# Attention with a top-32 mask and a feed-forward behind it: other places for values, feed-forward items and masking in each engine's queue

## The chip, the core and the metric

The kernel runs on one NeuronCore of one Trainium2 chip. Five engines with queues of their own work side by side: TensorE (PE; its weight loads are listed as PEld), VectorE (DVE), ScalarE (ACT), GpSimd (POOL) and SyncE (SP, which issues most transfers here). Each engine takes its instructions in the order in which the program issued them; an instruction that waits for another engine holds up all that stand behind it on its own. The metric is the device time of one execution in microseconds, as the median of several runs.

## What is computed

Eight batches of eight heads of attention, 576 rows of 64 each, keep the 32 largest scores of a row; the outcome goes through a feed-forward with the activation h - tanh(h). The weights come as 64-bit floats, all else is 32-bit.

```python
# q, k, v: (8, 8, 576, 64) float32
scores = scale * np.matmul(q, k.transpose(0, 1, 3, 2))
kth = np.partition(scores, -32, axis=-1)[..., -32:-31]
scores = np.where(scores >= kth, scores, -1e9)
attn = np.exp(scores - np.max(scores, axis=-1, keepdims=True))
attn = attn / (np.sum(attn, axis=-1, keepdims=True) + 1e-09)
x = np.matmul(attn, v)           # to (4608, 512): batch and row, then head and column
h = x @ w_in                     # (512, 2048)
return (h - np.tanh(h)) @ w_out  # (2048, 512)
```

## The kernel before

**Steps.** The attention is cut into 144 steps. A step is one pair of heads and a block of 128 rows (a `Step`); the 64 rows that are left over of each head make steps of their own, with two pairs of heads together (`rem`). The first batch, 18 steps, has `pe` set: its masked scores are transposed on PE. In the others DVE transposes them in blocks of 32 and 16 transfers on SP put the blocks in place (`turn_z`, `spread_keys`).

**What happens to a step n.** The work is spread over several turns of the loop in `run`, so that in each turn several steps are in the air:
- `scores(n)`, in turn n - 1: PE multiplies queries and keys into the one PSUM tile `scps`, ACT copies it to `sc`.
- `search(n)`, in turn n: DVE takes the minimum and maximum of two halves (L267, L268; these read `scps` and `sc` and write `ab`), then four rounds of the eight largest (L275) and their removal (L278). After each round `between` lets other work in: the conversion of weights (`convert`, L157 to L172, in turns 0 to 10 alone), transposes of keys and queries (L222), `turn_z`.
- `mask(n)`, in turn n + 1: POOL makes the threshold `tb` (L294) and the bias `nb` (L303); ACT computes a large value where a score is below the threshold (L307), POOL subtracts it (L310), once for each head. POOL then looks, from `ab`, whether a row may have been searched wrongly (`bad`, L314). `ab` has two buffers, so the search after the next one needs it.
- `expo(n)`, in turn n + 1: ACT takes the exponentials and their sums (L330), POOL adds a small number (L340).
- `turn_pe(n)`, in turn n + 2, for `pe` steps: nine transposes on PE (L409), eight at once and one behind `next(w)`, and ACT's copies to `et` (L412).
- `spread(n)`: POOL repeats the inverted sums along 64 columns (`rx`, L355).
- `values(n)`, in turn n + 2 for `pe` steps and n + 4 for the others, after the last step of a pair (or the only one): PE multiplies `et` with the values (L433), two heads beside each other in 64 columns, and transposes `rx` (L441); ACT copies both to `xs` (L445) and POOL multiplies them into `xT` (L457). `et` has one buffer: the next transfers into it wait until these matmuls have read it.

**The feed-forward.** Rows are gathered into units of 256 (128 at the start and for left-over rows). When the last values of a unit are made, its items are appended to the list `work`: `ffn_h` items (L486, 16 matmuls of 128 columns or 8 of 256 each in the program), of which each second one ends a PSUM tile `hps` that ACT turns into tanh (L498) and a copy `g` (L499) and POOL into `g` minus tanh (L500); then `ffn_o` items (L507, two matmuls of 512 columns), of which each eighth ends with ACT's copy `ot` (L517) and the transfer out. In the trace a float32 matmul stands as two instructions.

**Dealing.** `rate` looks at the number of items in `work` and at the turns in which later units will be ready, and says how many items this turn should do (`share`). `deal(part)` adds that part of the share to a credit and takes so many items from the list. The parts of a turn add up to 1.

**The order of a turn**, which sets the order in every queue: `spread(n - 3)`; `values`; `share`; the first eight transposes of `turn_pe(n - 2)`; `mask(n - 1)`; `search(n)`; `spread_keys(n - 2)`; for `pe` steps `spread(n - 2)`; `deal(0.4)`; `scores(n + 1)`; the ninth transpose; `expo(n - 1)`; `deal(0.2)`; `values(n - 2)` for `pe` steps; `deal(0.2)`; loads that are due; `deal(0.2)`. After the last turn the rest of the items follows in a row.

The pools matter where they make something wait: `scps` one tile; `zt` (which holds zt and av) two; `hps` and `ops` two together; `th` four, shared by tanh, `ot` and the conversion's `f`.

Of the kernel before, what the change touches and what calls it, by code (L numbers as in the profile page):

```python
# [8 lines left out]
AF = mybir.ActivationFunctionType  # L9
ALU = mybir.AluOpType  # L10
FP32 = mybir.dt.float32
# [5 lines left out]
BIG = 2.0**80  # L17
# [31 lines left out]
def kernel(  # L49
# [9 lines left out]
    nc = tc.nc  # L59
    P = nc.NUM_PARTITIONS  # L60
    B, H, S, D = q.shape
# [9 lines left out]
    NG = P // G  # L71
    KC = 2 * S // P
    G = 32
    NG = P // G
# [17 lines left out]
    zpool = pool("z", 2)  # L92
# [191 lines left out]
    def mask(n, exact):  # L284

        x = st[n]
        sc, m = x["sc"], x.pop("m")
        scf = sc[:].rearrange("p t s k -> p t (s k)")
        tb = mpool.tile([P, 2], FP32, tag="tb", name="tb")
        if exact:  # L290
            nc.gpsimd.tensor_scalar(tb[:], m[:, :, TOP - 1], BIG, None, ALU.mult)
        else:
            for t in range(2):
                nc.gpsimd.tensor_scalar(  # L294
                    tb[:, t : t + 1],
                    m[:, t, TOP - 1 : TOP],
                    m[:, t, TOP - 9 : TOP - 8],
                    BIG,
                    ALU.min,
                    ALU.mult,  # L300
                )
        nb = mpool.tile([P, 2], FP32, tag="nb", name="nb")
        nc.gpsimd.tensor_scalar(nb[:], m[:, :, 0], -scale, None, ALU.mult)  # L303
        z = zpool.tile([P, 2 * S], FP32, tag="z", name="z")
        zv = z[:].rearrange("p (t k) -> p t k", t=2)
        for t in range(2):
            nc.scalar.activation(  # L307
                zv[:, t, :], scf[:, t, :], AF.Relu, bias=tb[:, t : t + 1], scale=-BIG
            )
            nc.gpsimd.tensor_tensor(zv[:, t, :], scf[:, t, :], zv[:, t, :], ALU.subtract)  # L310
        if not exact:
            ab = x.pop("ab")
            for t in range(2):
                nc.gpsimd.tensor_scalar(  # L314
                    bad[:, t, n : n + 1],
                    ab[:, t, S2 + 7 : S2 + 8],
                    BIG,
                    tb[:, t : t + 1],
                    ALU.mult,
                    ALU.is_gt,  # L320
                )
        x.update(z=z, zv=zv, nb=nb)

    rds = {}
# [94 lines left out]
    def values(n):  # L419

        g = steps[n]
        nq, u = g.nq, g.unit
        et = tiles(ets.pop(n), nq)
        rx = rxs.pop(n)
        w = nq * P
        av = zt_ps.tile([P, 2, N], FP32, tag="zt", name="av")
        for i in range(2 if g.rem else 1):
            cols = half(i) if g.rem else slice(0, w)
            es = et[:, 2 * i : 2 * i + 2] if g.rem else et
            hp = g.hp + i  # L430
            for c in range(J + 1):
                for t in range(2):
                    nc.tensor.matmul(  # L433
                        av[half(t), 0, cols],
                        vb[g.b, hp][:, t, c, :] if c < J else vr[g.b, hp][:, t, :],
                        es[:, :, (J + 1) * t + c if c < J else J].rearrange("p a i j -> p a (i j)"),
                        start=(c == 0),
                        stop=(c == J),
                    )
        for i in range(nq):  # L440
            nc.tensor.transpose(  # L441
                av[:, 1, 0:w].rearrange("p (a i j) -> p i a j", a=NG, i=nq)[:, i], rx[:, i].rearrange("p t d -> p (t d)"), ident[:]
            )
        xs = xrpool.tile([P, 2, N], FP32, tag="xs", name="xs")
        nc.scalar.copy(xs[:, :, 0:w], av[:, :, 0:w])  # L445
        if g.rem:
            for i in range(2):
                nc.gpsimd.tensor_tensor(
                    xt(u)[:, g.hp + i, g.col : g.col + R],
                    xs[:, 0, half(i)],  # L450
                    xs[:, 1, half(i)],
                    ALU.mult,
                )
        else:

            xv = xs[:, :, 0:w].rearrange("p s (a i j) -> p s i a j", a=NG, i=nq)
            nc.gpsimd.tensor_tensor(  # L457
                xt(u)[:, g.hp, g.col : g.col + w].rearrange("p (i a j) -> p i a j", a=NG, i=nq),
                xv[:, 0],
                xv[:, 1],  # L460
                ALU.mult,
            )
        if n in done:
            work.extend(ffn(u))
# [6 lines left out]
            u.xT = p.tile([P, CD, N], FP32, tag=u.tag, name=u.tag)  # L471
        return u.xT

    cur = {}

    def ffn_h(u, item):

        w = u.n
        per = 2 * P // w
        for f in range(item * per, (item + 1) * per):  # L480
            j, fo = f // FJ, (f % FJ) * P
            s = f * w % 512
            if s == 0:
                cur[u] = h_ps.tile([P, 512], FP32, tag="h", name="hps")
            for c in range(CD):
                nc.tensor.matmul(  # L486
                    cur[u][:, s : s + w],
                    w_in[j][:, c, fo : fo + P],
                    u.xT[:, c, 0:w],
                    start=(c == 0),  # L490
                    stop=(c == CD - 1),
                )
        if item % 2:
            th = thpool.tile([P, 512], FP32, tag="th", name="th")
            if item % 4 == 1:
                u.g.append(gpool.tile([P, 2, 512], FP32, tag="g", name="g"))
            g = u.g[-1][:, item % 4 // 2, :]
            nc.scalar.activation(th[:], cur[u][:], AF.Tanh)  # L498
            nc.scalar.copy(g, cur[u][:])  # L499
            nc.gpsimd.tensor_tensor(g, g, th[:], ALU.subtract)  # L500

    def ffn_o(u, i, part):
        if part == 0:
            cur[u] = h_ps.tile([P, DM], FP32, tag="h", name="ops")
        for f in range(2 * part, 2 * part + 2):
            o = f * u.n + i * P
            nc.tensor.matmul(  # L507
                cur[u][:],
                u.g[o // 1024][:, o % 1024 // 512, o % 512 : o % 512 + P],
                w_out[f // FJ][:, f % FJ, :],  # L510
                start=(f == 0),
                stop=(f == CF - 1),
            )
        if part < CF // 2 - 1:
            return
        ot = thpool.tile([P, DM], FP32, tag="th", name="ot")
        nc.scalar.copy(ot[:], cur[u][:])  # L517
        for rows, dst in u.blocks[i]:
            nc.sync.dma_start(dst, ot[rows, :])
# [50 lines left out]
    def run(exact):  # L570
# [67 lines left out]
        def here(i):  # L638
            return 0 <= n + i < NS
# [24 lines left out]
        def rate():  # L664


            have, low, high = len(work), 0.0, None
            coming = sorted((t, u.n // 8) for u, t in ready.items() if t > n)
            for t, k in coming + [(NS + 4, 0)]:
                r = have / max(t - n, 1)  # L670
                high = r if high is None else min(high, r)
                have += k
            for u, t in begun.items():
                if t > n and u in before:
                    need = [i + 1 for i, x in enumerate(work) if x[1] is before[u]]
                    if need:
                        low = max(low, need[-1] / (t - n))
            return max(low, high)
# [11 lines left out]
        for n in range(-4, NS + 4):  # L690
            pe = here(-2) and steps[n - 2].pe
            if here(-3) and not steps[n - 3].pe:
                spread(n - 3)
            for m in (n - 4, n - 3):
                if 0 <= m < NS and steps[m].last and steps[m].lag == n - m:
                    values(m)
            share, usable = rate(), converted[0]
            if pe:
                w = turn_pe(n - 2)
                next(w)  # L700
            if here(-1):
                mask(n - 1, exact)
            if here(0):
                search(n, exact, between)
            elif here(-2):
                between(0)
            if here(-2) and not pe and steps[n - 2].last:
                spread_keys(n - 2)
            if pe:
                spread(n - 2)  # L710
            deal(0.4)
            if here(1):
                scores(n + 1)
            if pe:
                next(w)
            if here(-1):
                expo(n - 1)
            deal(0.2)
            if pe and steps[n - 2].last:
                values(n - 2)  # L720
            deal(0.2)
            for fn in todo.pop(n, []):
                fn()
            deal(0.2)
# [48 lines left out]
```

## Time and profile before

| | us |
|---|---|
| median of 5 runs | 1549.71 (1549.24 to 1550.34) |
| the profiled execution | 1551.08 |
| its span, first to last instruction | 1549.2 |
| PE busy | 1440.5 (93%) |
| DVE busy | 1347.2 (87%) |
| POOL busy | 943.2 (61%) |
| ACT busy | 884.0 (57%) |

Busy time is the time in which at least one record of the engine is open. A matmul's record begins before the one ahead of it has ended, so that PE's busy share can hide pauses of a tenth of a microsecond; how fast PE goes is read from the starts. The largest groups are `ops` on PE (L507, 522.9 us), `hps` on PE (L486, 474.4 us), the maxima on DVE (L275, 472.7 us), POOL's subtraction (L310, 400.5 us) and DVE's removals (L278, 382.6 us).

In the timelines below the columns are start, length, engine, line, operation, written and read tile, shape, count, and in brackets how long the engine had been idle before it and who ended that.

### The profile page before, as it was taken

What the parts mean: (1) busy time and instruction counts of PE and PEld (TensorE: products, weight loads), DVE (VectorE), ACT (ScalarE), POOL (GpSimd) and SP (SyncE); (2) the same over time, 40 slices, a digit from 0 to 9 for tenths busy, and PEclk for the clock granted to TensorE, in tenths of its full rate; (3) what the DMA queues carried; (4) which work ended last, traced back from release to release, by engine and by line L of the source; (5) the groups of instructions that cost most, each with busy time, mean ns of one, the idle gap of its engine ahead of it and who ended that gap; (6) DMA issues with size and microseconds to landing.
All of it is one profiled execution on the core that took longest, in us unless ns stands there. A gap on an engine that the chain in (4) does not pass through costs nothing.

```text
span 1549.2 us, 25298 instructions
## 1 busy us (share of the span) xinstructions
PE 1440.5 (93%) x7428; PEld 913.3 (59%) x7428; DVE 1347.2 (87%) x3828; ACT 884.0 (57%) x1567; POOL 943.2 (61%) x1525
## 2 busy tenths in 40 slices
PE   2566899899999999999999999999999999999997
PEld 1355567455566665656566665656566665656673
DVE  6997889999999999999999999999999999997300
ACT  4886767556555565656565565656565565655320
POOL 2777667667565675657565675757565675746420
PEclk9887899999999999999999999999999999999999
DMA  9944113324443354234433354334443344322200
GB/s 240 363 170 162 50 27 66 92 69 93 109 90 79 81 105 102 70 79 95 107 86 79 81 108 101 70 79 97 100 90 80 80 100 109 81 64 58 74 9 16
DMA packets 258836, 147.42 MB, mean 95 GB/s; under 512 B 210049, under 2 KB 217217, under 8 KB 258689
## 3 DMA queue, kind: packets, MB, share of 16 engines
q1 hardware_dynamic: 256912, 145.49, 38.4%
q8 instruction: 62, 1.02, 0.3%
q14 instruction: 86, 0.70, 0.2%
q10 hardware_dynamic: 1776, 0.22, 0.1%
HBM read 61.85 MB, written 9.44 MB: 46 GB/s over the span
## 4 chain that ended last, share of the span: by engine, by line
PE 73%; DVE 9%; SPq 6%; ACT 4%; issue 3%; DMA 3%; POOL 2%; DVEq 0%; ACTq 0%; POOLq 0%
PE ops L507 27%; PE hps L486 26%; PE av L433 9%; PE scps L237 8%; SPq L390 4%; DVE m L275 3%; DVE ab L278 2%; PE av L441 2%; SPq L200 1%; DMA zx<-in_moe_w_in_dram 1%; ACT z L307 1%; PE zt L409 1%; DVE ab L270 1%; DVE spare L376 1%; ACT f L158 1%
## 5 line engine op out<-in xcount | busy, mean ns | idle before, releaser
L507 PE MATMUL ops<-w_out,g 128*128 128x512 f32 x1152 | 522.9, 600 | 0.0
L486 PE MATMUL hps<-xT,w_in 128*128 128x256 f32 (+1 forms) x2176 | 474.4, 373 | 1.2 <-POOL xT L457 1.2
L275 DVE MAX8 m<-ab 128x8 f32<-128x288 f32 (+1 forms) x1152 | 472.7, 459 | 0.0
L310 POOL TENSOR_TENSOR z<-sc,z 128x576 f32<-128x576 f32 x288 | 400.5, 1412 | 84.0 <-ACT z L307 84.0
L486 PEld LDWEIGHTS hps<-xT,w_in 128*128 128x128 f32 x2176 | 393.1, 194 | 73.4 <-issue 22.5
L278 DVE MATCH_REPLACE8 ab<-m,ab 128x288 f32<-128x288 f32 x864 | 382.6, 459 | 0.0
L507 PEld LDWEIGHTS ops<-w_out,g 128*128 128x128 f32 x1152 | 211.3, 191 | 242.7 <-issue 239.1
L307 ACT ACTIVATE z<-sc,tb 128x576 f32<-128x576 f32 x288 | 207.9, 770 | 154.0 <-POOL tb L294 154.0
L500 POOL TENSOR_TENSOR g<-g,th 128x512 f32<-128x512 f32 x144 | 184.1, 1279 | 122.6 <-ACT g L499 107.2
L330 ACT ACTIVATE z<-z,nb 128x576 f32<-128x576 f32 x288 | 221.7, 774 | 7.2 <-POOL z L310 7.1
L245 ACT COPY sc<-scps 128x1152 f32<-128x1152 f32 x144 | 161.0, 1118 | 112.6 <-PE scps L237 108.8
L237 PE MATMUL scps<-kT,qT 64*128 64x288 f32 (+1 forms) x1280 | 185.0, 438 | 29.8 <-DVE qT L222 27.3
L433 PE MATMUL av<-et,vb 128*64 128x256 f32 (+1 forms) x1088 | 132.0, 378 | 44.5 <-ACT et L412 36.7
L237 PEld LDWEIGHTS scps<-kT,qT 64*128 64x128 f32 (+1 forms) x1280 | 100.3, 181 | 121.2 <-issue 58.9
L267 DVE TENSOR_TENSOR ab<-scps,sc 128x576 f32<-128x576 f32 x144 | 109.2, 758 | 69.4 <-POOL bad L314 59.3
L498 ACT ACTIVATE th<-hps 128x512 f32<-128x512 f32 x144 | 85.5, 594 | 107.7 <-PE hps L486 105.4
L457 POOL TENSOR_TENSOR xT<-xs 128x256 f32<-128x256 f32 (+1 forms) x68 | 47.3, 696 | 160.9 <-ACT xs L445 160.7
L445 ACT COPY xs<-av 128x512 f32<-128x512 f32 (+1 forms) x84 | 44.2, 526 | 164.6 <-PE av L441 164.4
L433 PEld LDWEIGHTS av<-et,vb 128*64 128x64 f32 x1088 | 75.3, 139 | 103.3 <-ACT et L412 38.8
L340 POOL TENSOR_SCALAR rd<-den 128x2 f32<-128x2 f32 x144 | 33.5, 233 | 143.7 <-ACT z L330 100.2
L270 DVE MAX8 ab<-ab 128x8 f32<-128x288 f32 x288 | 118.1, 457 | 0.0
L268 DVE TENSOR_TENSOR ab<-scps,sc 128x576 f32<-128x576 f32 x144 | 109.1, 757 | 0.0
(67 smaller groups left out, 1269.9 us busy)
## 6 DMA issues: line engine op xcount, KB each, us to landing
et<-spare SPq DMA_DIRECT2D x448, 72.0 KB, 2.0
et<-zx SPq DMA_DIRECT2D x448, 72.0 KB, 2.0
kin<-in_k_dram SPq DMA_DIRECT2D x116, 72.0 KB, 2.5
vb<-in_v_dram SPq DMA_DIRECT2D x64, 128.0 KB, 2.5
out_dram<-ot SPq DMA_DIRECT2D x32, 256.0 KB, 2.2
qin<-in_q_dram SPq DMA_DIRECT2D x113, 72.0 KB, 2.4
w_out<-in_moe_w_in_dram SPq DMA_DIRECT2D x10, 512.0 KB, 5.6
w_out<-in_moe_w_in_dram SPq DMA_DIRECT2D x10, 511.5 KB, 6.3
```

Of the source, the lines that this page charges most:

```text
L237: nc.tensor.matmul(ps[rows, t, s, 0:S2], qT[g.b, g.hp + i][half(t), qs], kT[g.b, g.hp + i][half(t), ks], start=True, stop=True,)
L245: nc.scalar.copy(sc[:], ps[:, :, :, 0:S2])
L270: nc.vector.max(ab[:, t, S2 : S2 + 8], lo[:, t, :])
L275: nc.vector.max(m[:, t, m8], last[t] if i == rounds - 1 else cur[t])
L278: nc.vector.match_replace(nxt[t], m[:, t, m8], cur[t], NEG)
L307: nc.scalar.activation(zv[:, t, :], scf[:, t, :], AF.Relu, bias=tb[:, t : t + 1], scale=-BIG)
L310: nc.gpsimd.tensor_tensor(zv[:, t, :], scf[:, t, :], zv[:, t, :], ALU.subtract)
L330: nc.scalar.activation(x["zv"][:, t, :], x["zv"][:, t, :], AF.Exp, bias=x["nb"][:, t : t + 1], scale=scale, accum_out=den[:, t : t + 1],)
L433: nc.tensor.matmul(av[half(t), 0, cols], vb[g.b, hp][:, t, c, :] if c < J else vr[g.b, hp][:, t, :], es[:, :, (J + 1) * t + c if c < J els ...
L486: nc.tensor.matmul(cur[u][:, s : s + w], w_in[j][:, c, fo : fo + P], u.xT[:, c, 0:w], start=(c == 0), stop=(c == CD - 1),)
L500: nc.gpsimd.tensor_tensor(g, g, th[:], ALU.subtract)
L507: nc.tensor.matmul(cur[u][:], u.g[o // 1024][:, o % 1024 // 512, o % 512 : o % 512 + P], w_out[f // FJ][:, f % FJ, :], start=(f == 0), sto ...
```

## The change

It has five parts.
- `mask` issues the row checks (`bad`) ahead of ACT's mask and POOL's subtractions.
- `ffn_h` no longer issues the subtraction of tanh from `g`; it notes it, and `finish` issues what was noted: right behind the mask of the next turn, or ahead of the first `ffn_o` item of a block.
- In a turn `mask` and `finish` now come ahead of `turn_pe`, and `values` for steps of the later batches come behind `deal(0.4)`, right ahead of `scores(n + 1)`.
- For those steps the transposes of `rx` come ahead of the values' matmuls.
- In turns with `pe` the dealing is 0, 0.8, 0 and 0.2 in place of 0.4, 0.2, 0.2 and 0.2: the 0.8 stands ahead of `values(n - 2)`.

`share` is computed where it was, which is now ahead of `values` for the later batches.

```diff
@@ mask
         nc.gpsimd.tensor_scalar(nb[:], m[:, :, 0], -scale, None, ALU.mult)
-        z = zpool.tile([P, 2 * S], FP32, tag="z", name="z")
-        zv = z[:].rearrange("p (t k) -> p t k", t=2)
-        for t in range(2):
-            nc.scalar.activation(
-                zv[:, t, :], scf[:, t, :], AF.Relu, bias=tb[:, t : t + 1], scale=-BIG
-            )
-            nc.gpsimd.tensor_tensor(zv[:, t, :], scf[:, t, :], zv[:, t, :], ALU.subtract)
         if not exact:
             ab = x.pop("ab")
...
+        z = zpool.tile([P, 2 * S], FP32, tag="z", name="z")
+        zv = z[:].rearrange("p (t k) -> p t k", t=2)
+        for t in range(2):
+            nc.scalar.activation(
+                zv[:, t, :], scf[:, t, :], AF.Relu, bias=tb[:, t : t + 1], scale=-BIG
+            )
+            nc.gpsimd.tensor_tensor(zv[:, t, :], scf[:, t, :], zv[:, t, :], ALU.subtract)
         x.update(z=z, zv=zv, nb=nb)
@@ values
+        def repeat_sums():
+            for i in range(nq):
+                nc.tensor.transpose(
+                    av[:, 1, 0:w].rearrange("p (a i j) -> p i a j", a=NG, i=nq)[:, i], rx[:, i].rearrange("p t d -> p (t d)"), ident[:]
+                )
+        if not g.pe:
+            repeat_sums()
         for i in range(2 if g.rem else 1):
...
-        for i in range(nq):
-            nc.tensor.transpose(
-                av[:, 1, 0:w].rearrange("p (a i j) -> p i a j", a=NG, i=nq)[:, i], rx[:, i].rearrange("p t d -> p (t d)"), ident[:]
-            )
+        if g.pe:
+            repeat_sums()
@@ feed-forward
-    cur = {}
+    cur, unfinished = {}, []
+
+    def finish():
+        for g, th in unfinished:
+            nc.gpsimd.tensor_tensor(g, g, th[:], ALU.subtract)
+        unfinished.clear()
@@ ffn_h
-            nc.gpsimd.tensor_tensor(g, g, th[:], ALU.subtract)
+            unfinished.append((g, th))
@@ ffn_o
         if part == 0:
+            finish()
@@ run
-            for m in (n - 4, n - 3):
-                if 0 <= m < NS and steps[m].last and steps[m].lag == n - m:
-                    values(m)
             share, usable = rate(), converted[0]
+            if here(-1):
+                mask(n - 1, exact)
+            finish()
             if pe:
                 w = turn_pe(n - 2)
                 next(w)
-            if here(-1):
-                mask(n - 1, exact)
...
-            deal(0.4)
+            deal(0.0 if pe else 0.4)
+            for m in (n - 4, n - 3):
+                if 0 <= m < NS and steps[m].last and steps[m].lag == n - m:
+                    values(m)
             if here(1):
                 scores(n + 1)
             if pe:
                 next(w)
             if here(-1):
                 expo(n - 1)
-            deal(0.2)
+            deal(0.8 if pe else 0.2)
             if pe and steps[n - 2].last:
                 values(n - 2)
-            deal(0.2)
+            deal(0.0 if pe else 0.2)
```

## The prediction

> **What bounds the kernel now.** The page's slices come first, because this kernel has stages with different limits.
>
> ```profile
> PE   2566899899999999999999999999999999999997
> DVE  6997889999999999999999999999999999997300
> PEclk9887899999999999999999999999999999999999
> ```
>
> A slice is 38.7 us. From the fifth on (155 us) TensorE is nearly always busy; before that it is half busy and its granted clock falls to 0.7. In the last two slices TensorE works alone: the feed-forward of the last unit. So the end is TensorE's total work plus the time in which it waits, and that waiting lies at the start. PE is busy 1440.5 of 1549.2 us; of the 108.7 us of idle time, some 82 lie ahead of 175 us by the table of stages. Next, that table, cut at the starts of searches 7 to 11 (the first vector operation of each), with ACT's and PE's timelines there:
>
> ```profile
> 100.63:116.64 16.01, 8.68 (x64) 7.71 (x64) 12.88 (x35) 12.17 (x24) 11.71 (x15) 0.86 0.57 200
> 116.64:133.03 16.39, 12.21 (x86) 10.85 (x86) 12.85 (x34) 12.02 (x24) 12.17 (x15) 0.81 0.39 129
> 133.03:150.17 17.14, 11.25 (x63) 8.77 (x64) 12.74 (x34) 12.81 (x25) 12.07 (x15) 0.70 0.47 172
> 150.17:170.32 20.15, 12.37 (x38) 5.81 (x35) 14.14 (x37) 12.81 (x24) 10.99 (x14) 0.75 0.31 105
> ```
>
> ```profile
> 116.76 0.48 PE L433 MATMUL av<-et,vb 128*64 128x128 f32 x1 [5.69 <-ACT et L412]
> ...
> 118.42 3.62 PE L486 MATMUL hps<-xT,w_in 128*128 128x128 f32 x16
> 121.83 1.39 PE L409 MATMUL zt<-ident,z 128*128 128x128 f32 x8
> ```
>
> ```profile
> 118.66 0.37 ACT L445 COPY xs<-av 128x256 f32<-128x256 f32 x1 [0.43 <-PE av L441]
> 122.88 1.07 ACT L412 COPY et<-zt 128x512 f32<-128x512 f32 x2 [3.85 <-PE zt L409]
> 123.84 1.45 ACT L307 ACTIVATE z<-sc,tb 128x576 f32<-128x576 f32 x2
> 125.18 0.72 ACT L158 ACTIVATE f<-f,e 128x512 f32<-128x512 uint32 x1
> ```
>
> The columns of the first fence are length, then busy time of PE, PEld, DVE, ACT and POOL, clock, DMA. No engine fills these steps: it is a loop. PE waits 5.69 us for the last copy of ACT (et), finishes the values, then does one feed-forward item (3.4 us at the lowered clock) and only then the transposes zt. ACT stands 3.85 us for those, and its mask (L307), the three weight conversions from L158 on and the scores' copy queue behind.
>
> In steps 12 to 15 the search waits for the row check:
>
> ```profile
> 204.66 0.76 DVE L267 TENSOR_TENSOR ab<-scps,sc 128x576 f32<-128x576 f32 x1 [2.85 <-POOL bad L314]
> ```
>
> From 225 to about 440 us DVE has no gap: a step takes 8.76 us, or 9.44 with a key or query transpose (start to start of L267). After that PE is the limit:
>
> ```profile
> 566.43 1.95 PE L433 MATMUL av<-et,vb 128*64 128x256 f32 x16
> 568.21 0.60 PE L433 MATMUL av<-et,vr 128*64 128x256 f32 x4
> 568.74 0.44 PE L441 MATMUL av<-ident,rx 128*128 128x128 f32 x2
> 569.02 3.60 PE L507 MATMUL ops<-w_out,g 128*128 128x512 f32 x8
> 572.54 1.24 PE L237 MATMUL scps<-kT,qT 64*128 64x288 f32 x8
> 573.72 7.13 PE L507 MATMUL ops<-w_out,g 128*128 128x512 f32 x16
> ```
>
> A matmul's record overlaps the next one's, so starts are read, not lengths: 64 ops in a row take 0.429 us each in the tail; here eight take 572.54 - 569.02 = 3.52, that is 8 x 0.429 + 0.09.
>
> **The change part by part.** All is summed against the profiled execution (1551.08 us, span 1549.2); the difference is then put on the median 1549.71.
>
> *Items ahead of the values, first 18 steps.* By the listing of both programs' PE instructions, in steps 6 to 9 the before has one item between values and the next zt each time. The after keeps it at the ends of steps 6 and 8 alone; two items stand ahead of the values, in PE's waits of 5.69, 3.91 and 5.49 us, at no cost. If they overran that wait, xs would be late by the overrun; each takes 1.8 us at full clock, 3.4 at the lowered one.
>
> The price is the time from the end of xs to the first conversion (L158). Before: 5.51 us in step 7 (103.28 to 108.79), 6.15 in step 8, 7.20 in step 9, 6.25 in step 10. After, the mask comes ahead of turn_pe, so ACT's order is mask, et: xT 0.46, first tb 0.45, masks 1.34, et 0.96 and some 0.3 of handing over: 3.5 us where zt waits for no item (steps 8, 10). With an item left in step 7, zt's first half is ready 3.3 us after xs, then et 1.07: 4.35. Step 9 follows the last item of a pair, whose tanh and copy stand ahead of the mask on ACT (138.5 + 1.05, then 1.34 and 0.96): 6.6. Gains: 1.2 + 2.6 + 0.6 + 2.7 = **7.1**. In steps 3 to 6 there is no item; the time is 3.17 us (65.34 to 68.51), so the new order costs 0.33 x 4 = 1.3. Sum: **5.8 gained**. Bounds: ACT's idle time in the four steps (3.84 + 4.37 + 4.33 + 7.34 = 19.9) if all went; below nothing by 4 x 1.44, if the et copies, now behind two masks, became what the step waits for. I take the sum because each of its terms has a row.
>
> A rule bears on the 3.4 us. The rows show 16 hps in 3.4 us here and in 1.79 at 188 us, where the granted clock is 1.0. The Trainium skill (TensorE: Matmul & The Clock Gate, Part 1) says that PE falls to half clock after an idle window of about 3.4 us. Moving an item of 1.8 us into the waits leaves about 3.9, 2.1 and 3.7. By the rule two of them straddle the window; were the clock kept, the two items left would give 1.6 us more each: 9 instead of 5.8. I keep the row.
>
> *Row checks ahead of the subtractions, deferred g.* The check frees ab for the search after next. It moves ahead of 2 x 1.41 us of subtractions, into POOL's wait for ACT's mask; that delays the first subtraction by up to 0.65 us, hidden by expo's place behind the scores' copy. The three waits in steps 12 to 15 (1.08 + 2.85 + 1.11) go: **5.0 gained**. Next late is DVE itself: steps 11 to 22 took 95.5 us, its own work is 89.7. From 225 us the check's other waits (45 us between 450 and 1375) lie under PE's work: nothing. The g subtraction (1.28) leaves POOL's way ahead of tb and waits up to a step; its reader comes items later. Without that cover ops would wait 1.28 each time.
>
> *Sums' transposes, values, scores in a row.* Before, a values group changes PE's tile form four times with its scores: full to 128*64, back, full to 64*128, back. Leaving the values costs, in starts, 0.310 instead of 0.209 to the first transpose and 0.164 instead of 0.107 to the second: 0.157. After, one return is gone and 128*64 goes straight to 64*128. The trace has no such pair. If that were free, another 0.19 would go (0.093 before the scores, 0.34 instead of 0.24 within); the Trainium skill (TensorEngine Tiling (Array Packing), Key Properties) speaks against it: changing the mode, not just the tile, drains the engine. So one change is saved, not two: 57 groups from step 42 on x 0.157 = **9.0 gained** (19.8 by the lenient reading, 0 if this direct change cost double). The 13 earlier ones lie in DVE's stage.
>
> *Where values stand.* rx is a step old and et's 16 DMAs (10.01 us on SP, 2.0 to land) are issued once the previous values have read et; both move by the same 0.4 of a share, so their distance stays about 19 us. SP holds the loads queued behind by up to 3.5 us; they are needed steps later. I cost it nothing (7.8 us of PE's waits for et and q DMAs might go, a few be added).
>
> *The dealing.* Not in the words of the change: the share is now computed before values() adds a finished unit's items, so such a step deals less and later ones more. In the listing the before alternates 8.3 and 10.9 us of PE work per step; the after has steps of 3.1, 4.4, 6.2, 4.8 (13 under 7.5 us against 2). I summed steps 22 to 143: scores start when PE gets there, but 1.5 us after the previous search's start at the earliest (L268 frees the bank); a search starts 2.57 us after its scores and not before DVE's 8.76 or 9.44. For the before this gives 1415.0 at search 142 (trace: 1422.7; 5 of the difference arises before step 46) and 7.3 us of waiting PE; for the after 16.3. **9.0 lost**, nearly all by step 46; later PE's lead of up to 4.7 us (8.76 - 1.5 - 2.57) carries the light steps. The tail has 5 items more and stays full.
>
> Sum: -5.8 - 5.0 - 9.0 + 9.0 = -10.8: **1538.9 us**.
>
> **The rivals.** *Dealing wins (slower).* PE has no lead to live on: if the time from scores to search grew from 2.57 to beyond 5 us, as the copy queues behind more work on ACT, light steps would cost their whole deficit: 66.5 us against 37.8, so 28.7 lost in place of 9.0: 1549.7 + 28.7 - 9.0 - 10.8 = 1559. It decides from 20 us of extra waiting. For it: 13 light steps. Against: searches start 2.6 us after scores throughout, with ACT 57% busy. *The loop finds another wait.* ACT's wait for zt becomes one for POOL's tb, as long, and nothing is gained early: -9.0 + 9.0, 1549.7, no change. For it: tb takes 1.87 us at 120.18, behind xT. Against: without that row's g subtraction it starts earlier. *More comes early.* ACT becomes the bound of steps 7 to 10 with 1.1 us idle in each: 19.9 - 4.4 = 15.5, less 1.3, and 5.8: 1529.7.
>
> **How the numbers follow.** Forecast 0.52 (own range 1532 to 1546), dealing 0.20, no early gain 0.12, more early 0.16. Under 0.2%, 3.1 us, a measurement of this kernel can't tell a difference from none. Faster: 0.50 + 0.16 + 0.04 = 0.70; same 0.10; slower 0.20. The range 1526 to 1556 leaves out half of the slower case and a third of the fastest.
>
> **What would show it.** Right: searches 7 to 11 about 13 to 17 us apart, ACT's wait for zt gone in two of four; no wait of L267 for bad; search 22 about 11 us earlier; transposes with no gap ahead of the values; PE idle by 9 us more between 260 and 480 us. Wrong: steps 7 to 10 as long as now, or PE idle again and again beyond 500 us.

## The result, and the profile after

The changed kernel took 1552.0 us (median; 1550.2 to 1555.0), the kernel before beside it 1549.9 (1546.6 to 1553.5). The ratio is 1.0016, with a 95% interval of 1.0011 to 1.0021: within 0.2%, on the slower side. 1538.9 was forecast. So the question is where 11 us of expected gain went.

The profiled execution of the changed kernel is its longest on record: 1559.07 us, 7.1 above the median, with a span of 1557.2. It lies 8.0 us over the profiled execution before, where the medians are 2.1 apart, so some of what its first 170 us show belongs to that execution alone; e2 and e6 below have profiled executions within 0.5 us of their medians and are the better witnesses there. First, the page's slices of the changed kernel (38.9 us each; busy tenths, and the granted clock):

```profile
PE   1566799979989999999999999999999999999997
...
DVE  6988899999999999999999999999999899888100
...
PEclk9868799999999999999999999999999999999999
```

The shape has stayed: TensorE half busy until about 155 us, then nearly always busy. The stages, cut at the start of search 11, of search 22, of the last score matmul and of the last feed-forward matmul, say more (profiled executions, us; all kernels of the experiments are in it):

| kernel | to search 11 | 11 to 22 | 22 to last scores | tail | ending | span |
|---|---|---|---|---|---|---|
| before | 170.3 | 95.5 | 1166.8 | 105.4 | 11.2 | 1549.2 |
| **after** | 175.4 | 96.7 | 1160.7 | 114.0 | 10.4 | 1557.2 |
| e1 items first | 164.1 | 96.0 | 1166.1 | 105.4 | 10.6 | 1542.2 |
| e2 checks first | 177.1 | 93.9 | 1164.9 | 105.4 | 10.8 | 1552.1 |
| e3 in a row | 167.6 | 95.5 | 1158.3 | 114.0 | 10.5 | 1545.8 |
| e4 in a row, even share | 166.9 | 96.7 | 1153.0 | 107.2 | 7.6 | 1531.5 |
| e5 after, even share | 172.2 | 96.8 | 1151.0 | 107.2 | 7.6 | 1534.8 |
| e6 after, checks last | 164.7 | 97.1 | 1159.0 | 114.0 | 10.3 | 1545.1 |
| e7 after, rx early | 162.3 | 96.7 | 1158.2 | 114.0 | 10.7 | 1541.9 |
| e8 checks twice | 171.1 | 95.1 | 1165.0 | 105.4 | 10.3 | 1546.9 |
| e9 checks first late | 168.9 | 93.3 | 1166.9 | 105.4 | 10.7 | 1545.3 |
| e10 the parts that gain | 162.9 | 93.4 | 1151.0 | 107.2 | 7.5 | 1522.0 |
| e11 the same, rx early | 155.9 | 93.8 | 1151.1 | 107.2 | 7.6 | 1515.5 |
| e12 after, three mends | 165.0 | 97.0 | 1151.0 | 107.2 | 7.5 | 1527.8 |

From search 22 on, changed and unchanged kernel take nearly the same (1285.1 and 1283.4 us), as forecast. Nearly all of the miss lies ahead of it: in this execution search 22 comes 6.3 us later, not 10.8 earlier. Here are steps 7 to 10 of the changed kernel, cut as before (length, then busy time of PE, PEld, DVE, ACT and POOL, clock, DMA):

```profile
107.32:123.24 15.92, 12.38 (x86) 10.96 (x86) 13.21 (x35) 11.76 (x21) 10.78 (x14) 0.79 0.58 198
123.24:139.09 15.85, 9.51 (x70) 7.88 (x70) 15.25 (x35) 13.29 (x26) 11.83 (x14) 0.88 0.36 132
139.09:158.09 19.00, 12.31 (x62) 8.75 (x62) 15.14 (x35) 12.43 (x23) 12.56 (x15) 0.77 0.45 161
158.09:175.45 17.36, 10.72 (x30) 5.61 (x30) 14.02 (x38) 12.04 (x20) 10.74 (x14) 0.70 0.36 122
```

They sum to 68.1 against 69.7 us: 1.6 gained in place of 7.1. The column to look at is DVE's: it runs 34 to 38 instructions in each of these steps, as before, yet in the second and third it is busy 15.25 and 15.14 us where it was 12.85 and 12.74. The same instructions have become longer. In the second, two conversions of weights take 1.5 us each, where all six of that step took 0.41 to 0.43 before; POOL's row, given behind DVE's two, is the deferred subtraction of tanh:

```profile
132.14 1.49 DVE L157 TENSOR_SCALAR f<-spare 128x512 uint32<-128x512 uint32 x1
133.56 1.48 DVE L163 TENSOR_SCALAR w_out<-spare 128x512 uint32<-128x512 uint32 x1
```

```profile
131.63 1.72 POOL L486 TENSOR_TENSOR g<-g,th 128x512 f32<-128x512 f32 x1
```

Steps 3 to 6 took 54.7 us against 50.1.

The waits of the search for the row check are gone, but another wait stands in their place. These are the views of DVE's waits from 175 to 240 us (total, times, longest), before and then after:

```profile
DVE ab L267 <- POOL bad L314: 5.0, 3, 2.9
```

```profile
DVE ab L267 <- ACT sc L245: 5.7, 5, 2.0
```

### The profile page after: what moved, and what is told of

Same layout as the page of the kernel before. It is cut to its first block, busy times and chain, and to the rows that moved or that the text cites. A ratio compares the mean times of both kernels' runs of the same rounds, so it can differ in the third digit from the quotient of the medians.

```text
span 1557.2 us, 25234 instructions
## 1 busy us (share of the span) xinstructions
PE 1437.1 (92%) x7428; PEld 927.4 (60%) x7428; DVE 1353.7 (87%) x3828; ACT 876.7 (56%) x1567; POOL 936.0 (60%) x1525
## 4 chain that ended last, share of the span: by engine, by line
PE 77%; DVE 9%; SPq 4%; ACT 3%; DMA 2%; issue 2%; POOL 2%; DVEq 0%; ACTq 0%; POOLq 0%
PE hps L499 30%; PE ops L521 27%; PE av L443 9%; PE scps L237 9%; SPq L390 3%; DVE m L275 2%; DVE ab L278 2%; SPq L200 1%; PE av L430 1%; DVE f L169 1%; ACT z L318 1%; PE zt L409 1%; DMA zx<-in_moe_w_in_dram 1%; DVE ab L267 1%; DVE ab L268 1%
## 5 line engine op out<-in xcount | busy, mean ns | idle before, releaser
L521 PE MATMUL ops<-w_out,g 128*128 128x512 f32 x1152 | 516.4, 599 | 2.2 <-POOL g L486 2.2
L499 PE MATMUL hps<-xT,w_in 128*128 128x256 f32 (+1 forms) x2176 | 465.8, 372 | 0.6 <-POOL xT L465 0.5
L321 POOL TENSOR_TENSOR z<-sc,z 128x576 f32<-128x576 f32 x288 | 400.5, 1413 | 90.1 <-ACT z L318 90.1
L237 PE MATMUL scps<-kT,qT 64*128 64x288 f32 (+1 forms) x1280 | 190.6, 449 | 37.2 <-DVE qT L222 28.7
L267 DVE TENSOR_TENSOR ab<-scps,sc 128x576 f32<-128x576 f32 x144 | 108.7, 755 | 63.1 <-ACT sc L245 59.5
L268 DVE TENSOR_TENSOR ab<-scps,sc 128x576 f32<-128x576 f32 x144 | 109.1, 758 | 0.0
```

The costliest lines, as they stand in the source:

```text
L237: nc.tensor.matmul(ps[rows, t, s, 0:S2], qT[g.b, g.hp + i][half(t), qs], kT[g.b, g.hp + i][half(t), ks], start=True, stop=True,)
L268: nc.vector.tensor_tensor(hi, ps[:, :, 0, 0:S2], sc[:, :, 1, :], ALU.max)
L499: nc.tensor.matmul(cur[u][:, s : s + w], w_in[j][:, c, fo : fo + P], u.xT[:, c, 0:w], start=(c == 0), stop=(c == CD - 1),)
L521: nc.tensor.matmul(cur[u][:], u.g[o // 1024][:, o % 1024 // 512, o % 512 : o % 512 + P], w_out[f // FJ][:, f % FJ, :], start=(f == 0), sto ...
```

## The experiments

Two theories at the start. **A**: the parts that were to gain do, alone, and the row checks ahead of the mask cost something on POOL or DVE in the early steps. **B**: the early loop is bound elsewhere, so that no part gains there. A third question was whether the forecast's two 9.0 us cancel because both are right. Each time below is a median beside the median of the kernel before on the same chip in the same series (1547.83 for e1 to e4, 1549.14 for e6 to e9, 1548.96 for the others).

**e1, items first.** The dealing of `pe` turns alone, in the kernel before:

```diff
-            deal(0.4)
+            deal(0.0 if pe else 0.4)
...
-            deal(0.2)
+            deal(0.8 if pe else 0.2)
             if pe and steps[n - 2].last:
                 values(n - 2)
-            deal(0.2)
+            deal(0.0 if pe else 0.2)
```

> The kernel before with the new dealing of the pe steps alone (0, 0.8, 0, 0.2). Theory A (a closed loop of conversions, rx, values, xs, tb and mask sets steps 3 to 10, and the item between values and zt is a part of it): two of the four items leave the loop, searches 8 and 10 come 2.5 to 3.5 us sooner each, 1543 to 1546 us. Theory B (the items were never a part of the loop, ACT's wait for zt becomes another as long): 1549 to 1551 us. Theory C (the early loss of the changed kernel is chance of the first transfers): no statement, but then e1, e2 and the kernel before start search 7 within 2 us of each other.

1542.57 us, ratio 0.9968 (0.9956 to 0.998): 5.3 faster. By stages of e1, cut near the starts of searches 7 to 11:

```profile
100.10:116.00 15.90, 11.19 (x86) 10.05 (x86) 12.78 (x35) 11.88 (x23) 11.66 (x14) 0.89 0.58 199
116.00:129.80 13.80, 10.29 (x72) 8.22 (x70) 12.86 (x35) 12.24 (x24) 11.67 (x14) 0.75 0.43 156
129.80:147.20 17.40, 11.97 (x63) 8.62 (x62) 12.80 (x35) 13.06 (x26) 12.12 (x15) 0.79 0.48 171
147.20:164.10 16.90, 10.40 (x34) 5.39 (x31) 14.16 (x38) 12.77 (x24) 10.98 (x14) 0.80 0.36 126
```

Steps 8 and 10 are 2.6 and 3.3 us shorter than in the kernel before; steps 7 and 9 stay. DVE's busy time is what it was. The items alone bring nearly the 5.8 us that the forecast gave them together with the mask ahead of `turn_pe`.

**e2, checks first.** The row checks ahead of the mask alone, in the kernel before:

```diff
         nc.gpsimd.tensor_scalar(nb[:], m[:, :, 0], -scale, None, ALU.mult)
+        if not exact:
+            ab = x.pop("ab")
...
         z = zpool.tile([P, 2 * S], FP32, tag="z", name="z")
...
-        if not exact:
-            ab = x.pop("ab")
```

> The kernel before with the row checks ahead of the subtractions alone. Theory A (the checks had kept POOL busy while DVE's L163 ran; now POOL's weight multiplication runs against it and L163 takes 1.5 us for 0.4): searches 3 to 10 come 0.5 to 1 us later each, 4 to 7 us in all; the three waits for bad in steps 12 to 15 go, 5 us gained: 1548 to 1553 us, with L163 slow once a step. Theory B (the loss comes from the mask ahead of the et copies): no step 3 to 10 is longer, and the 5 us are gained: 1544 to 1546 us.

1554.23 us, ratio 1.0045 (1.0031 to 1.0058): 6.4 slower, where a gain of 5.0 was forecast for this part. Search 11 comes 6.8 us late, and steps 3 to 6 take 13.2, 13.5, 13.5 and 14.5 us against 12.7, 12.2, 12.3 and 13.0, almost what the changed kernel shows (13.2, 14.1, 13.2, 14.3). One place in step 5 explains it. First the kernel before, DVE's timeline and then POOL's:

```profile
82.84 0.51 DVE L157 TENSOR_SCALAR f<-w_out 128x512 uint32<-128x512 uint32 x1
83.28 0.41 DVE L163 TENSOR_SCALAR w_in<-w_out 128x512 uint32<-128x512 uint32 x1
```

```profile
80.28 2.79 POOL L310 TENSOR_TENSOR z<-sc,z 128x576 f32<-128x576 f32 x2 [1.37 <-ACT z L307]
83.07 0.98 POOL L314 TENSOR_SCALAR bad<-ab,tb 128x1 uint8<-128x1 f32 x2
84.00 1.26 POOL L172 TENSOR_TENSOR w_in<-w_in,f 128x512 f32<-128x512 f32 x1
```

And e2 (L321 is the subtraction there):

```profile
83.42 0.83 DVE L157 TENSOR_SCALAR f<-w_out 128x512 uint32<-128x512 uint32 x1
84.17 1.49 DVE L163 TENSOR_SCALAR w_in<-w_out 128x512 uint32<-128x512 uint32 x1
```

```profile
81.19 2.77 POOL L321 TENSOR_TENSOR z<-sc,z 128x576 f32<-128x576 f32 x2
83.92 1.44 POOL L172 TENSOR_TENSOR w_in<-w_in,f 128x512 f32<-128x512 f32 x1
```

Before, POOL's two small checks stand between its subtractions and its first weight multiplication (L172), 83.07 to 84.05, just while DVE does L157 and L163. The multiplication begins when DVE is back at its maxima. In e2 that gap is empty. L172 starts at 83.92 and ends at 85.36; L163, which by its record begins at 84.17, ends at 85.66, that is 0.30 us behind L172. L157 ends at 84.25, 0.29 behind the subtractions' end at 83.96. So DVE does not go slower beside POOL, it stands until POOL is through. The same holds throughout: in the traces of all fourteen kernels 94 instructions of L157 and L163 take more than 0.6 us, and each ends 0.28 to 0.31 us behind the end of a subtraction or multiplication on POOL. The list of L163's durations (shortest, median, longest, in ns) shows the effect for the weights that go from `w_out` to `w_in`, in the kernel before and then in e2:

```profile
L163 DVE TENSOR_SCALAR w_in<-w_out x10: 414/421/428, 10.2 to 83.3; 128x512 uint32<-128x512 uint32 x10
```

```profile
L163 DVE TENSOR_SCALAR w_in<-w_out x10: 411/422/1486, 9.2 to 84.2; 128x512 uint32<-128x512 uint32 x10
```

Over all 32 conversions, seven L163 in e2 take 1.48 to 1.50 us and none does before: 7 x 1.07 = 7.5 us. Steps 3 to 10 of e2 are 8.5 us longer than before (54.8 + 73.5 against 50.1 + 69.7; its first three were 1.7 shorter). The changed kernel has seven such L163 too, and in steps 8 and 9 an L157 of 1.49 and 1.50 us behind the deferred subtraction.

The Trainium skill has the rule (SBUF — State Buffer, Who interferes with whom): VectorE and GpSimd share a pair of ports; a `tensor_scalar` of VectorE can enter a mode that takes it, and whichever starts second is blocked until the first has ended. The rows agree to 0.3 us. They don't show who started first: in the kernel before L172 is the one that stands at 46.57, with 1.65 us instead of 1.27, beside an L163 of 0.41 whose record begins 0.11 us later. The rule also fits POOL's two checks, which take 0.98 us beside L157 and L163 and 0.56 in e2, where DVE is elsewhere.

**e8, the checks twice.** If the checks were a spacer, then putting a second, useless pair back at the old place should repair e2 although it adds work (the edit, against e2):

```diff
             nc.gpsimd.tensor_tensor(zv[:, t, :], scf[:, t, :], zv[:, t, :], ALU.subtract)
+        if not exact and n < 10:
+            for t in range(2):
+                nc.gpsimd.tensor_scalar(
+                    bad[:, t, n : n + 1],
...
```

> The kernel before with the row checks ahead of the mask, as in e2, and in the ten steps with weight conversions computed a second time at their old place behind the subtractions: more work for POOL than in either. Theory A (collision): with the checks gone from behind the subtractions, POOL's first weight multiplication starts while DVE is in L157 and L163, and these wait until it has ended (L163 1.49 us in place of 0.41 in e2). The second pair of checks, about 0.9 us, stands where that pair stood before, so L163 is back near 0.4 us, steps 3 to 6 near 12.2 to 13.0 us, and the time within 1.5 us of the kernel before, 6 us under e2. Theory B (POOL's own queue is late: subtractions, multiplications and the repeated sums behind them): 0.9 us more in each of ten steps makes it slower still, 1555 to 1561.

1546.76 us, ratio 0.9984 (0.9975 to 0.9993): 2.4 us under the kernel before, where e2 was 6.4 over it. More work, and 8.8 us less time when each is set against the kernel before of its own series (7.5 between the two medians); even a little less than theory A had it. The timelines of e8, DVE and POOL:

```profile
83.84 0.51 DVE L157 TENSOR_SCALAR f<-w_out 128x512 uint32<-128x512 uint32 x1
84.28 0.41 DVE L163 TENSOR_SCALAR w_in<-w_out 128x512 uint32<-128x512 uint32 x1
```

```profile
84.05 0.97 POOL L324 TENSOR_SCALAR bad<-ab,tb 128x1 uint8<-128x1 f32 x2
84.99 1.26 POOL L172 TENSOR_TENSOR w_in<-w_in,f 128x512 f32<-128x512 f32 x1
```

The second pair stands beside L157 and L163, L163 is back at 0.41 and so is every other one; steps 3 to 6 take 12.7, 12.2, 12.5 and 13.0. That a POOL queue which is late could be the cause (theory B of this run, 1555 to 1561) is out.

**e9, checks first late.** The checks ahead of the mask from turn 11 on (`n >= 10` in `mask`), when no weights are left to convert.

> The kernel before with the row checks ahead of the mask only from the turn on in which no weights are converted any more. Theory A: the early loss of e2 (about 7 us by search 11) does not appear, and what e2 gained between searches 11 and 22 (1.6 us) does: 1.0 to 2.5 us faster than before. By the prediction's own term it would be 5.0 faster. Theory B (the checks ahead of the mask delay POOL's subtraction and with it the exponentials in all steps): no gain, or up to 2 us slower.

1546.8 us, ratio 0.9985 (0.9975 to 0.9994): 2.3 faster. Nothing is lost early, and searches 11 to 22 take 93.3 us in place of 95.5: 2.2 gained, not 5.0. The reason stands in e2's timeline too, at the search that had waited 2.85 us for the check:

```profile
210.19 0.76 DVE L267 TENSOR_TENSOR ab<-scps,sc 128x576 f32<-128x576 f32 x1 [1.85 <-ACT sc L245]
```

L267 waits for two things. With the check early, the scores' copy is what is late, and of 2.85 us only 1.0 went.

**e6, the changed kernel with the checks last again.**

> The changed kernel with the row checks back behind the subtractions; all else as changed. If the parts add up (items ahead -5.3, checks ahead +6.4, values in a row about +1), it takes 6 us less than the changed kernel, 5 less than before: 1542 to 1546, with steps 3 to 6 back to 12.2 to 13.0 us. If the mask ahead of turn_pe and the deferred subtraction of tanh are what costs the early steps, 1548 to 1552, with steps 3 to 6 still above 13.

1547.28 us, ratio 0.9989 (0.9979 to 0.9998). Steps 3 to 6 are back at 12.7, 12.6, 12.1 and 13.0 us, so the mask ahead of `turn_pe` costs next to nothing there. But 1.9 faster than before is less than the 3.8 that e1 and e3 make together, and the two parts that e6 adds to those, the mask's place and the deferred subtraction, show in the trace. Step 17 takes 10.2 us against 8.2 before, and not in e1 or e3. Four L163 and one L157 take 1.48 to 1.62 us, the L157 behind the deferred subtraction. And ACT's waits in steps 7 to 10 change place. In e1:

```profile
ACT et L412 <- PE zt L409: 5.0, 5, 3.5
```

In e6:

```profile
ACT xs L453 <- PE av L430: 6.2, 4, 3.0
ACT z L307 <- POOL tb L294: 3.4, 4, 0.9
...
ACT et L412 <- PE zt L409: 1.2, 1, 1.2
```

The wait for `zt` has gone down, but those for `av` and for POOL's `tb` have grown (2.7 and 0.9 us in e1), and PE's wait for `rx` ahead of `av` is 10.1 us against 6.2. Steps 7 to 10 take 66.3 us in e6 and 64.0 in e1. Which of the two parts does how much of this was not separated.

**e3, in a row,** the third part alone: `values` of the later batches behind `deal(0.4)`, the transposes of `rx` ahead of their matmuls, and so the share computed before a finished unit's items are in the list.

```diff
-            for m in (n - 4, n - 3):
-                if 0 <= m < NS and steps[m].last and steps[m].lag == n - m:
-                    values(m)
             share, usable = rate(), converted[0]
...
             deal(0.4)
+            for m in (n - 4, n - 3):
+                if 0 <= m < NS and steps[m].last and steps[m].lag == n - m:
+                    values(m)
```

> The kernel before with the sums' transposes, values and scores in a row alone, the share computed ahead of the values as in the changed kernel. Prediction's sum: 9.0 us gained by one change of tile form less, 9.0 lost by the dealing, from search 22 on: 1548 to 1552 us; searches up to 11 within 1 us of the kernel before. Rival (the new place of the values costs by itself, by waits for et): 1555 us or more.

**e4, the same with an even share:** the items that the coming `values` will add are counted.

```diff
-            share, usable = rate(), converted[0]
+            fresh = sum(
+                steps[m].unit.n // 8
+                for m in (n - 4, n - 3)
+                if m in done and steps[m].lag == n - m
+            )
+            share, usable = rate(fresh), converted[0]
...
-            have, low, high = len(work), 0.0, None
+            have, low, high = len(work) + fresh, 0.0, None
```

> e3 with the share counting the items of the units that become ready in this turn, as the kernel before does. If the dealing costs what the sum says, 6 us less than e3 (idle PE 10 us for 16, 7 light steps for 13): 1542 to 1546 us. If the light steps cost nothing: as e3.

e3 took 1549.32 us, ratio 1.0008 (0.9999 to 1.0018): no difference, as forecast for gain and dealing together. e4 took 1534.26, ratio 0.9914 (0.9901 to 0.9928). So the even share is worth 15 us in the new order, and what the uneven one hides is a gain larger than 9. The longest of PE's waits from 260 to 1420 us are (total, times, longest), before,

```profile
PE av L433 <- DMA et<-spare: 4.2, 4, 2.1
PE av L433 <- DMA et<-zx: 3.2, 2, 1.7
```

in e3

```profile
PE scps L237 <- DVE ab L268: 7.5, 5, 4.6
PE av L441 <- DMA spare<-zx: 3.1, 3, 2.1
PE scps L237 <- ACT z L307: 2.2, 1, 2.2
```

and in e4

```profile
PE scps L237 <- DVE ab L268: 5.2, 4, 2.0
PE av L441 <- DMA qin<-in_q_dram: 2.2, 2, 1.8
```

Light steps make PE wait for the score bank (L268), once for 4.6 us. What PE doesn't do then is left for later, in the end for the tail: 114.0 us in e3, 107.2 in e4. Most of it has arisen by search 46, as these lists of the `ops` matmuls from search 22 to search 46 show, e3 and then e4:

```profile
L513 PE MATMUL ops<-w_out,g x167: 592/592/1220, 278.7 to 483.3; 128*128 128x512 f32 x167
```

```profile
L513 PE MATMUL ops<-w_out,g x188: 592/592/1222, 279.5 to 483.2; 128*128 128x512 f32 x188
```

All other matmuls are equally many, and the stretch is 1.1 us longer in e3; 21 `ops` at 0.429 us are 9.0 us of work, so some 10 us are lost by then. Together, from search 22 to the last matmul, e4 is 12.1 us shorter than e3 and 12.0 shorter than before. Another 2.9 us come from the ending, and these the even share has over the kernel before as well, so they are no price of the uneven dealing against it. The matmul of the closing row check (`cnt`) stood behind all others before; in e4 it stands 58 us ahead of the end of the tail. Before, and then e4:

```profile
L737 PE MATMUL cnt<-ones,anybad x2: 163/164/164, 1538.5 to 1538.5; 128*1 128x1 f32 x2
```

```profile
L748 PE MATMUL cnt<-ones,anybad x2: 164/164/164, 1466.3 to 1466.3; 128*1 128x1 f32 x2
```

All programs that count the coming items end 7.5 or 7.6 us after the start of the last feed-forward matmul, all others 10.3 to 11.2. This shows where the 2.9 us are; that the place of `cnt` is their cause, and why it comes earlier there, was not tested.

**e5, the changed kernel with the even share.**

> The changed kernel, with one more term in its share: the items of a unit that the coming values will finish in the same turn are counted, as they were before the change. By the prediction's sum the uneven dealing costs 9.0 us: 1542 to 1544. By e3 against e4 it costs 15, of which 11.8 are pauses of PE between search 22 and the last matmul: 1535 to 1539.

1535.26 us, ratio 0.9908 (0.9893 to 0.9923): the even share is worth as much in the changed kernel, 15.8 us (13.7 under its own kernel before, where the changed kernel was 2.1 over), again with 2.8 of it in the ending.

**e7, the changed kernel with rx early:** `spread(n - 2)` for `pe` steps right behind `invert` in `between`, ahead of the weight multiplications.

> The changed kernel with the repeated sums of the first 18 steps (rx on POOL) issued right behind DVE's inversion, ahead of the weight multiplications instead of behind them. Theory L (a closed loop: DVE's L169, two multiplications of 2.6 us, rx, the transposes on PE, xs, xT, tb, the mask, the conversions, L169): PE's wait for rx, 13.8 us from 60 to 175 us, falls to under 5, steps 3 to 8 are 0.4 to 1.0 us shorter each, the time 1545 to 1549. Theory A alone (DVE waits for POOL's multiplication at L163 and nothing else): the stall stays at 1.4 us a step and the time at 1550 to 1553.

1543.14 us, ratio 0.9955 (0.994 to 0.9969), better than either theory had it. In the changed kernel PE waits for `rx` (PE's waits from 60 to 175 us, total, times, longest):

```profile
PE av L443 <- ACT et L412: 24.7, 7, 5.2
PE av L430 <- POOL rx L355: 13.8, 7, 3.3
```

In e7 the second line is gone from that view, and steps 7 to 10 take 60.7 us in place of 68.1. `rx` between the subtractions and L172 is also a spacer of a kind: one L163 over 1.4 us is left of seven, though eight L157 now take more than 0.6 us, where it was four. The two effects were not separated in e7; e11 does it.

**e10, the parts that gain,** in the kernel before: e1, e9, and e4. **e11:** e10 with rx early.

> The kernel before with the parts that gained: items ahead of values in the first 18 steps (e1, -5.3), checks ahead of the mask from turn 11 on (e9, -2.4), values behind the first part of the dealing with the sums' transposes ahead of them and the even share (e4, -13.6). If the parts add up, 21 us under the kernel before: 1526 to 1530. If the early gains are taken up by DVE's stage behind them, as far as 225 us and beyond, 1530 to 1535.

> e10 with the repeated sums (rx) of the first 18 steps ahead of the weight multiplications, as in e7. If PE's wait for rx lies on the loop without the collision too (3.6 us before, 10.7 in e6), 2 to 5 us under e10. If it only counted because the collision had made POOL late, within 1 us of e10.

e10 took 1523.65 us, ratio 0.9836 (0.9822 to 0.9849), and e11 1518.14, ratio 0.9806 (0.9793 to 0.9819). The parts add up and more: 25.3 against 21; where the rest comes from was not followed up. rx early brings 5.5 in a kernel in which no L163 collides with or without it, so PE's wait for `rx` lies on the early loop by itself. Both beat the kernel before and the changed one.

**e12, the changed kernel with three mends** (checks first from turn 11 on, rx early, even share). Against e11 it has the mask ahead of `turn_pe` and the deferred subtraction.

> The changed kernel with three mends: checks ahead of the mask only from turn 11 on, rx early, the even share. Against e11 it differs in the mask ahead of turn_pe and the deferred subtraction of tanh. If those two cost what steps 16 and 17 show (8.65 and 10.16 us in e6 against 8.26 and 8.15 before, 2.4 in all), it is 1 to 4 us over e11. If they gain where ACT no longer waits in steps 7 to 10, it is at or under e11.

1522.89 us, ratio 0.9841 (0.9818 to 0.9864), 4.8 over e11: these two parts cost, and more than steps 16 and 17 show. Its single executions lie in two groups, three from 1521.8 to 1522.9 and two at 1529.6 and 1530.9 us. The profiled one, at 1529.63, has eight L163 and nine L157 beyond 0.6 us, and all but one of these seventeen end behind a subtraction of the mask. Whether the shorter executions have fewer of them is not known, since they have no profile.

## Why the prediction was wrong, by its steps

Alone, three parts make -5.3 (e1), +6.4 (e2) and +1.5 us (e3), +2.6 in all; the changed kernel is 2.1 over the kernel before. That these agree is in part luck. The mask's new place and the deferred subtraction were never run alone; they cost 1.9 us by e6 and 4.8 by e12. In the changed kernel the early checks cost 4.0 (against e6), not 6.4. Each of these figures can be off by some 2 us. Of the four terms, -5.8, -5.0, -9.0 and +9.0, and the one put at nothing:

- **Items ahead of the values, -5.8: right for the items, wrong for the mask ahead of `turn_pe`.** e1, the items alone, has -5.3. Of the four steps, 8 and 10 gave 2.6 and 3.3 (2.6 and 2.7 forecast), 7 and 9 gave 0.1 and -0.3. PE has room for an item in its wait for `et`, and of ACT's 11.0 us of waits for `zt` in these steps 6.0 go. The forecast's 1.2 and 0.6 us in steps 7 and 9, less 1.3 in steps 3 to 6, came from the mask's new place; in e6 step 7 gains nothing, step 9 loses 1.6 us, and the waits for `av` and `tb` take over. Of the two values weighed for this part, 5.8 by the row of 3.4 us an item and 9 by the rule of the clock gate, the measurement is near the first; the granted clock of the four steps was 0.89, 0.75, 0.79 and 0.80 in e1, and 0.86, 0.81, 0.70 and 0.75 before.
- **Row checks ahead of the subtractions, -5.0: the step that failed, in sign (+6.4 in e2).** It held that moving the checks "delays the first subtraction by up to 0.65 us, hidden", and looked at what the move adds to POOL's queue. It did not ask what the moved instructions had been beside. They kept POOL's multiplication off DVE's two conversions, and without them DVE stood 1.07 us in each of seven steps, 7.5 us in all. The sentence "Next late is DVE itself" was wrong too: the scores' copy was next, and only 2.2 of the 5.0 us were gained (e9). The kernel before could have told it, by the row of the scores of that search:

```profile
200.22 1.24 PE L237 MATMUL scps<-kT,qT 64*128 64x288 f32 x8
```

By the forecast's own 2.57 us a search starts at 202.79 at the earliest; the wait began at 204.66 - 2.85 = 201.81. So at least 0.98 of the 2.85 us would remain whatever the check did; in e2 1.85 remained. The deferred subtraction of tanh, put at nothing in the same term, adds to the loss: it is what two of the long L157 stand behind.
- **One tile form less, -9.0: right in mechanism, confirmed in size.** The view below is PE's timeline of the changed kernel. From the first transpose to the end of the scores it takes 574.04 - 570.25 = 3.79 us. Before, values and transposes took 569.02 - 566.43 = 2.59, the scores 573.72 - 572.54 = 1.18, and each of the two was entered at a price of 0.09: 3.95. That is 0.16 us a group. The place is typical: over the groups from step 42 on the medians are 3.79 us for 44 groups after, and 2.59 and 1.17 before. The four matmuls of `vr` take 0.53 us to the start of what follows them, whether that is the full form (568.74 - 568.21) or the scores (572.87 - 572.34): the change from 128*64 to 64*128 costs as much as one to the full form, as the rule of the drain that the prediction cites has it. The lenient reading, 19.8, is out.

```profile
570.25 0.38 PE L430 MATMUL av<-ident,rx 128*128 128x128 f32 x2
570.56 1.95 PE L443 MATMUL av<-et,vb 128*64 128x256 f32 x16
572.34 0.60 PE L443 MATMUL av<-et,vr 128*64 128x256 f32 x4
572.87 1.24 PE L237 MATMUL scps<-kT,qT 64*128 64x288 f32 x8
574.04 8.90 PE L499 MATMUL hps<-xT,w_in 128*128 128x256 f32 x40
```

- **Where values stand, 0.** e4 is 12.0 us shorter than before from search 22 to the last matmul, 3 more than the tile forms. PE's waits for `et` and its transfers, 7.4 us before, are no longer in e4's view, which the forecast had named as what might go; all waits of that view sum to 12.8 us before and 9.5 in e4. That the new place alone does this was not tested.
- **The dealing, +9.0: right in kind and place, a third too small.** Against an even share it costs 12.1 us up to the last matmul, some 10 of them by search 46, where the forecast had "nearly all by step 46". That this is 3 too little and the term above 3 too little the other way is luck: the two cancel in the sum. The 2.9 us of the ending were in no term.

Of the rivals, the one that ended at 1549.7 came near the time, and has a part in the reason: a wait for `tb` does take over where the mask stands ahead (e6), but e1 shows that the items' gain is there, and the larger part of the miss is the checks. The dealing costs more than any other part, but no more than the order that causes it gains, so it did not decide the outcome. The rival "More comes early" has a slip: it adds the 5.8 that its 15.5 replaces, where the 5.0 of the checks belongs; the sum is 1530.5, not 1529.7.

## What to carry to other kernels

When an instruction is moved, look not only at what it will hold up at its new place but at what starts earlier where it stood: here VectorE's `tensor_scalar` of 128x512 and GpSimd's long operations could not run beside each other, and the one that stood was counted as busy, not as waiting. A wait that is removed is worth only the distance to the next of the same instruction's conditions, and both times stand in the trace of before. And where work is shared out by a count, look at when the count is taken: an order changed for another reason moved it here, and that cost as much as the order gained.

## What the runs showed that was not expected

- DVE's `tensor_scalar` of 128x512 takes 0.41 us, and 1.48 to 1.50 us in e2 where it stands behind POOL's multiplication of 128x512 (1.31 to 1.45 us there); it ends 0.30 us behind the multiplication. DVE's maxima and removals beside the same multiplication keep their length (before, from 83.61 us on: 0.81 for two maxima, 0.44 for a removal).
- Adding ten pairs of useless checks made a kernel 8.8 us faster (e8 against e2, each set against the kernel before of its series).
- In the kernels in which the closing check's matmul is not the last on PE, the ending is about 3 us shorter; a cause was not tested.
